# Second expert layer: an up-projection by seven products of halves instead of eight, on pairs of blocks

## The chip, the cores and the metric

The kernel runs on one core of one Trainium2 chip. The metric is the device time of one execution in microseconds, smaller is better. Three executions of the kernel before took 954.00, 954.44 and 953.73 us, median 954.0. The profiled execution took 954.2 us, with a span of 952.0 us from its first to its last instruction and a granted TensorE clock of 1.000 all the way.

## The reference

```python
q_p, k_p = phi(q * scale), phi(k * scale)        # exp of random features, 4 batches, 8 heads, 576 tokens
num = einsum('bhsm,bhmd->bhsd', q_p, einsum('bhsm,bhsd->bhmd', k_p, v))
den = einsum('bhsm,bhm->bhs', q_p, sum(k_p))[..., None] + 1e-06
x = (num / den), heads side by side               # 2304 tokens x 512
h = x @ moe_w_in                                  # first layer, 512 -> 2048
x = maximum(0.01 * h, h) @ moe_w_out              # 2048 -> 512
h = x @ moe2_w_in                                 # second layer, 512 -> 2048: the change is here
out = (h * clip(h + 3, 0, 6) / 6) @ moe2_w_out    # 2048 -> 512
```

All arrays are float32. Only `h` of the second layer, for token groups of 512, is computed in another way after the change.

## The kernel before

**Precision.** Every matrix product of the two layers is made from operands that are split into a high part, rounded to the type `F32R`, and a low part, the rest. `mm3` (L415 to L418) adds three matmuls: high by high, low by high, high by low. `copy_alts` makes the high part (ScalarE or VectorE, recorded at L409 and L408), `sub_alts` the low part (VectorE or GpSimd, L412 and L413).

**Groups and blocks.** The 2304 tokens are five groups, `GN = [512, 256, 512, 512, 512]`. Layer one takes them in this order, with the attention of the next group between the matmuls; layer two takes them as 0, 2, 3, 4, 1, so that the group of 256 is last. In `moe` (L715) a group goes over `FT` = 16 blocks of 128 hidden columns. `Hblk(j)` (L727) is the up-projection of a block: for each of the four slices of 128 input features (`xs[k]`, the split input) one `mm3` with the block's weights standing and the group's tokens moving, 12 matmuls into one PSUM bank. In layer two ScalarE then computes relu(h + 3) into a tile `u` (L742), VectorE computes min(u, 6) * h into the bank (L743), and the result is split into the two parts of `g` (L409, L748). `Oblk(j)` (L752) is the down-projection: `g` stands, the split `moe2_w_out` moves, 12 matmuls of 512 columns into four accumulator banks, two blocks behind `Hblk`. After the last block the four accumulators go through a scaled copy (`late_o`, L773) to the output.

**Weights.** `weight` (L435) loads one block of 512 KB by DMA into one of two buffers `wst`, turns 64-bit into 32-bit floats with four instructions (L444, L446, L449, L452), and splits it into a pair of tiles `w`. The split weights of a layer stay in SBUF for all five groups: 32 pairs of `w` are needed in each layer; seven further pairs (`NMORE`) become free when attention is over (`phase4`, L390), together with four output tiles `o`.

**The order of work.** Nothing is ordered by hand. Each operation goes to `Graph` with its possible engines and their planned costs, its buffers, and a due time. `Graph.run` repeatedly takes the operation that can start first by its own clock of the engines (due times decide between starts less than 60 ns apart), and writes the instructions in that order. An engine's cost is raised by `BIAS` when the planner chooses between engines (VectorE by 900 ns). Buffers of one tag are taken in the order of the program. Up-projection banks (`use` "H") may hold four of the eight PSUM banks at the end, accumulators (`acc`) four.

Of the kernel before, what the change touches and what calls it, by code (L numbers as in the profile page):

```python
# [24 lines left out]
KT = DM // 128  # L25
# [7 lines left out]
NMORE = 7  # L33
# [7 lines left out]
LEAD = 0.8  # L41
O1, O2 = 11e3, 12e3
EARLY2 = 60e3
T0, D1, D2 = 42e3, 100e3, 89e3
# [10 lines left out]
class Buf:  # L55
    __slots__ = ("tag", "slot", "left", "freed", "writers", "readers", "tiles", "first", "use", "phase")
    NOW = 0

    def __init__(self, tag, use=None):
# [9 lines left out]
class Graph:  # L69
# [6 lines left out]
    ANY = ("nm",)  # L76
    WHILE = {}
# [8 lines left out]
    def op(self, alts, rd=(), wr=(), due=0.0, also=()):  # L86
# [27 lines left out]
        for x in list(wr) + [(b, "new") for b in also]:  # L114
# [7 lines left out]
            if b.slot is None and b.tag is not None:  # L122
                b.slot = -1
                o.allocs.append(b)
                self.fifo.setdefault(b.tag, []).append(o.seq)
# [13 lines left out]
    def run(self, slots, spare, phase, later):  # L139
# [9 lines left out]
        turn = {t: 0 for t in self.fifo}  # L149
        held = {"acc": 0, "H": 0, "att": 0, "first": 0}  # L150
# [8 lines left out]
        while pend:  # L159
            best = None  # L160
            short = set()
            for o in sorted(pend, key=lambda o: (o.due, o.seq)):
# [5 lines left out]
                for b in o.allocs:  # L168
# [50 lines left out]
            for b in o.allocs:  # L219
# [9 lines left out]
                else:  # L229
                    turn[b.tag] += 1  # L230
            fn()
            done += 1
            for b in o.bufs:
                b.left -= 1
                b.freed = max(b.freed, o.end)
                if b.left == 0 and b.tag is not None:
# [3 lines left out]
                    if b.use is not None:  # L240
                        held[b.use] -= 1
            self.todo[o.phase] -= 1
# [58 lines left out]
def attn_moe_kernel(ctx: ExitStack, tc: tile.TileContext, qT, kT, qn, kn, v1, om2, w1i, w1o, w2i, w2o, out):  # L301
# [21 lines left out]
    x1 = [[dram.tile([128, GN[i]], F32, name=f"x1_{i}_{k}") for k in range(KT)] for i in range(NG)]  # L323
# [14 lines left out]
        "o": [],  # L338
# [75 lines left out]

    def mm3(o, ah, al, bh, bl, start, stop):  # L415
# [19 lines left out]
    def weight(src, j, due):  # L435
        st, t, w = Buf("wst"), Buf("wt"), Buf("w")
# [14 lines left out]
            rd=[(st, 1)], wr=[(st, 0)], due=due)  # L451
        g.op([("dve", c_dve(512), lambda: nc.vector.scalar_tensor_tensor(  # L452
# [262 lines left out]
    def moe(grp, second, wi, wo, T):  # L715
        n = GN[grp % NG]
        step = (D2 if second else D1) * n / 512.0 / (FT + 1.0)
        xs = [] if second or grp else [firstx[k] for k in range(KT)]
        for k in range(KT - len(xs)):
            xr, x = xraw[grp, k], Buf("x")  # L720
            g.op(copy_alts(lambda x=x: x.tiles[0][:, :n], lambda xr=xr: xr.tiles[0][:, :n], n), rd=[xr], wr=[(x, 0)], due=T - 1e3)
            g.op(sub_alts(lambda x=x: x.tiles[1][:, :n], lambda xr=xr: xr.tiles[0][:, :n], lambda x=x: x.tiles[0][:, :n], n), rd=[xr, (x, 0)],
                 wr=[(x, 1)], due=T - 1e3)
            xs.append(x)
        acc = [Ps("acc") for _ in range(n // 128 if second else KT)]

        def Hblk(j):  # L727
            p = Ps("H")
            P = lambda: p.tiles[0][:, :n]
            for k in range(KT):  # L730
                def mm(k=k):
                    wh, wl = win(wi[j], k)
                    mm3(P(), wh, wl, xs[k].tiles[0][:, :n], xs[k].tiles[1][:, :n], k == 0, k == KT - 1)
                g.op([("pe", 3 * c_mm(n), mm)], rd=[wi[j], xs[k]], wr=[p], due=T + step * (j - LEAD * (j == FT - 1)))
# [17 lines left out]
        def Oblk(j, gg):  # L752
            w = wo[j]
            for i, a in enumerate(acc):
                def mm(i=i, a=a):
                    c = slice(i * 128, i * 128 + 128)
                    if second:
                        mm3(a.tiles[0], gg.tiles[0][:, c], gg.tiles[1][:, c], w.tiles[0], w.tiles[1], j == 0, j == FT - 1)
                    else:
                        mm3(a.tiles[0][:, :n], w.tiles[0][:, c], w.tiles[1][:, c], gg.tiles[0][:, :n], gg.tiles[1][:, :n], j == 0, j == FT - 1)  # L760
                g.op([("pe", 3 * c_mm(512 if second else n), mm)], rd=[w, gg], wr=[a], due=T + step * (j + 1.6))

        gs = {}
        for j in range(FT + 2):
# [4 lines left out]
        for i, a in enumerate(acc):  # L769
            d = T + step * (FT + 1.0) - 4e3  # L770
            if second:
                o = Buf("o")
# [159 lines left out]
```

## Time and profile before

| | |
|---|---|
| median of three executions | 954.0 us (953.73 to 954.44) |
| the profiled execution | 954.2 us, span 952.0 us |
| TensorE busy | 945.0 us, 99% |
| weight loads on TensorE busy (beside matmuls) | 776.1 us |
| VectorE busy | 429.9 us, 45% |
| ScalarE busy | 423.4 us, 44% |
| GpSimd busy | 203.2 us, 21% |

In the profile, an instruction's time is its start to its end. Matmuls are pipelined: the time of one matmul reaches over the start of the next, so the distance from start to start is what a matmul takes from the engine. The same holds in smaller measure for the other engines. PE is TensorE, PEld its weight loads, DVE VectorE, ACT ScalarE, POOL GpSimd.

### The profile page before, as it was taken

The page shows a single profiled execution, that of the slowest core. Times are in us where ns is not written, and L with a number is a line of the kernel's source. Part 1 is how long each engine was busy: PE and PEld are TensorE (multiplying, and loading weights), DVE is VectorE, ACT ScalarE, POOL GpSimd, SP SyncE. Part 2 cuts the span into 40 slices and gives each one's busy share as a digit, 9 for nine tenths or more (in the row PEclk, how much of TensorE's full clock was granted, in tenths as well). Part 3 has the DMA queues.
Part 4 walks back from the last instruction along what each step waited for, and adds up shares of the span by engine and source line. Part 5 has one row for each costly group of instructions (what it writes and reads, how often), then busy time and mean ns, then how long its engine had stood idle before and what let it go on. Part 6 is the DMA issues. An engine that isn't in the chain of part 4 may idle for free.

```text
span 952.0 us, 13570 instructions
## 1 busy us (share of the span) xinstructions
PE 945.0 (99%) x5102; PEld 776.1 (82%) x5102; DVE 429.9 (45%) x1020; ACT 423.4 (44%) x964; POOL 203.2 (21%) x297
## 2 busy tenths in 40 slices
PE   9999999999999999999999999999999999999998
PEld 8878778899778877777888888888888888888897
DVE  6897978635722234124666663222222222222232
ACT  6867767655643344234545553232223223222332
POOL 2455445322410022012533421020002001000100
PEclk9999999999999999999999999999999999999999
DMA  9457545433201211000544450020002000100000
GB/s 328 131 160 233 186 141 156 117 91 97 64 26 55 60 45 56 1 1 1 199 133 133 123 187 22 1 89 1 1 0 89 1 1 11 55 1 1 29 17 23
DMA packets 38128, 72.92 MB, mean 77 GB/s; under 512 B 10032, under 2 KB 15280, under 8 KB 38064
## 3 DMA queue, kind: packets, MB, share of 16 engines
q1 hardware_dynamic: 38064, 72.07, 23.7%
q8 instruction: 40, 0.66, 0.3%
q14 instruction: 24, 0.20, 0.1%
HBM read 62.62 MB, written 9.44 MB: 76 GB/s over the span
## 4 chain that ended last, share of the span: by engine, by line
PE 97%; ACT 1%; DMA 1%; DVE 0%; issue 0%; SPq 0%; POOL 0%
PE bank L416 29%; PE bank L417 28%; PE bank L418 28%; PE bank L532 4%; PE bank L578 3%; PE bank L708 2%; PE bank L685 1%; PE bank L589 1%; PE bank L619 1%; ACT first_h L512 1%; DMA first_xn<-kn 1%; PE bank L553 0%; PE bank L610 0%; PE bank L637 0%; ACT ht L512 0%
## 5 line engine op out<-in xcount | busy, mean ns | idle before, releaser
L748 DVE TENSOR_TENSOR g<-bank,g 128x512 fp32r<-128x512 f32 (+1 forms) x160 | 101.7, 636 | 159.1 <-ACT g L409 158.3
L743 DVE SCALAR_TENSOR_TENSOR bank<-u,bank 128x512 f32<-128x512 f32 (+1 forms) x80 | 51.3, 642 | 230.0 <-ACT u L742 229.7
L742 ACT ACTIVATE u<-bank,three 128x512 f32<-128x512 f32 (+1 forms) x80 | 51.6, 645 | 198.2 <-PE bank L418 197.8
L416 PE MATMUL bank<-x,w 128*128 128x512 f32 (+1 forms) x340 | 127.3, 375 | 0.0
L418 PE MATMUL bank<-x,w 128*128 128x512 f32 (+1 forms) x340 | 125.3, 369 | 0.0
L417 PE MATMUL bank<-x,w 128*128 128x512 f32 (+1 forms) x340 | 125.2, 368 | 0.0
L409 ACT CAST g<-bank 128x512 fp32r<-128x512 f32 (+1 forms) x160 | 87.3, 546 | 50.9 <-DVE bank L743 49.4
L413 POOL TENSOR_TENSOR x<-xr,x 128x512 fp32r<-128x512 f32 (+1 forms) x36 | 42.5, 1203 | 309.7 <-ACT x L409 258.2
L746 ACT ACTIVATE bank<-bank 128x512 f32<-128x512 f32 (+1 forms) x80 | 43.7, 546 | 85.0 <-PE bank L418 84.2
L416 PEld LDWEIGHTS bank<-x,w 128*128 128x128 f32 x340 | 64.0, 188 | 15.1 <-issue 3.6
L416 PE MATMUL bank<-x,second_w 128*128 128x512 f32 (+1 forms) x200 | 76.0, 380 | 0.0
L501 DVE TENSOR_REDUCE nm<-bank 128x4 f32<-128x512 f32 (+3 forms) x92 | 49.5, 568 | 55.8 <-PE bank L532 55.0
L417 PE MATMUL bank<-x,second_w 128*128 128x512 f32 (+1 forms) x200 | 74.6, 373 | 0.0
L418 PE MATMUL bank<-x,second_w 128*128 128x512 f32 (+1 forms) x200 | 74.5, 373 | 0.0
L418 PEld LDWEIGHTS bank<-x,w 128*128 128x128 f32 x340 | 64.0, 188 | 10.9
L417 PEld LDWEIGHTS bank<-x,w 128*128 128x128 f32 x340 | 64.1, 188 | 10.6
L512 ACT ACTIVATE h<-bank,nm 128x128 f32<-128x128 f32 x208 | 58.6, 391 | 31.4 <-POOL nm L507 31.2
L416 PE MATMUL bank<-w,g 128*128 128x512 f32 x180 | 70.2, 390 | 0.0
L417 PE MATMUL bank<-w,g 128*128 128x512 f32 x180 | 70.2, 390 | 0.0
L418 PE MATMUL bank<-w,g 128*128 128x512 f32 x180 | 70.0, 389 | 0.0
L416 PE MATMUL bank<-g,w 128*128 128x512 f32 (+1 forms) x180 | 68.8, 382 | 0.0
L418 PE MATMUL bank<-g,w 128*128 128x512 f32 (+1 forms) x180 | 66.4, 369 | 0.0
(168 smaller groups left out, 1897.6 us busy)
## 6 DMA issues: line engine op xcount, KB each, us to landing
wst<-w2i SPq DMA_DIRECT2D x16, 512.0 KB, 3.6
wst<-w2o SPq DMA_DIRECT2D x16, 512.0 KB, 3.6
v<-v SPq DMA_DIRECT2D x14, 330.0 KB, 2.9
wst<-w1i SPq DMA_DIRECT2D x9, 512.0 KB, 4.8
wst<-w1o SPq DMA_DIRECT2D x9, 512.0 KB, 3.9
out<-late_o SPq DMA_DIRECT2D x18, 256.0 KB, 2.1
x<-u SPq DMA_DIRECT2D x16, 256.0 KB, 2.1
xr<-x SPq DMA_DIRECT2D x16, 256.0 KB, 2.8
```

The lines of the kernel that those rows point to most:

```text
L409: return [("act", c_act(n, psum), lambda: nc.scalar.copy(dst(), src())), dve if psum else dve + (True,)]
L413: ("pool", c_pool(n), lambda: nc.gpsimd.tensor_tensor(out=dst(), in0=src(), in1=hi().bitcast(F32), op=ALU.subtract))]
L416: nc.tensor.matmul(o, lhsT=ah, rhs=bh, start=start, stop=False)
L417: nc.tensor.matmul(o, lhsT=al, rhs=bh, start=False, stop=False)
L418: nc.tensor.matmul(o, lhsT=ah, rhs=bl, start=False, stop=stop)
L501: g.op([("dve", c_dve(c * 128), lambda raw=raw, n_=n_: nc.vector.tensor_reduce(out=n_()[:, :, 0], in_=raw(), axis=AX.X, op=ALU.min))], rd= ...
L512: nc.scalar.activation(h.tiles[0][:, q * 128:q * 128 + 128], raw()[:, q], AF.Exp, bias=nm.tiles[0][:, q], scale=-1.0)
L532: nc.tensor.matmul(ps[bank].tiles[0][o, i * 128:i * 128 + 128], lhsT=src.tiles[0][r, i * 128:i * 128 + n], rhs=wn[r], start=True, stop=True)
L742: g.op([("act", c_act(n, True, True), lambda: nc.scalar.activation(U(), P(), AF.Relu, bias=three))], rd=[p], wr=[u], due=d)
L743: g.op([("dve", c_dve(n), lambda: nc.vector.scalar_tensor_tensor(out=P(), in0=U(), scalar=6.0, in1=P(), op0=ALU.min, op1=ALU.mult))], rd=[ ...
L746: g.op([("act", c_act(n, True), lambda: nc.scalar.activation(P(), P(), AF.Prelu, alpha=0.01))], wr=[p], due=d)
L748: g.op([("dve", c_dve(n), lambda: nc.vector.tensor_tensor(out=G1(), in0=P(), in1=G0().bitcast(F32), op=ALU.subtract))], rd=[p, (gg, 0)], w ...
```

## The change

It concerns layer two alone, and there the four groups of 512 tokens (`fast`). Two blocks of hidden columns become a pair. The input (4 slices of 128 features by 512 tokens) and the pair's weights (4 slices by 256 hidden columns) are regarded as 2 x 2 matrices of halves: features halved into two slices each, tokens halved into 256 each, hidden columns halved into the two blocks. The four halves of the result come from seven products and a number of sums and differences, in place of eight products. Each product is two slices of `mm3` with 256 moving columns, that is, six matmuls. The sums are distributed thus:

- Input: for each group, four differences (`minus`) and seven splits (`xsplit`) replace four splits. Three of the split halves (`x2`) lie in `w` buffers.
- Weights: blocks of `moe2_w_in` stay unsplit (`raw`, two blocks to a buffer, in the space that attention leaves). For each pair in each group four sums or differences of 256 columns (`S`, in a `wst` buffer) and four splits (`c`, three of 512 columns and one of 256, in `w` buffers) are made anew. In the last group, of 256 tokens, each block is split anew as well, and its products stay as they were.
- Results: products that go into more than one half of the result are copied out of PSUM (`keep`) or added on the way out (`total`). Region `R[0]`, half a bank, is accumulated into by four products in turn, and is copied out after each of them, before the next may add to it.

```diff
-NMORE = 7
+NMORE = 3
+PAIRLAG = 2.0
+BIAS2 = 300.0
+EARLY3 = 20e3
+    CAP = {"c": 8, "x2": 3, "g2": 2}
...
-                    elif t not in self.ANY and self.fifo[t][turn[t]] != o.seq:
+                    elif t not in self.ANY and self.fifo[b.line][turn[b.line]] != o.seq:
+                        ok = None
+                        break
+                    elif lines[b.line] >= self.CAP.get(b.line, 99):
...
             if left == 0:
                 share["H"], share["att"], share["first"] = HSHARE, 0, 0
+                self.BIAS = dict(self.BIAS, dve=BIAS2)
...
-        a, x = room("late", [("o", 4, ([128, 512], F32)), ("w", NMORE, *wspec)], 0, side="right")
+        a, x = room("late", [("raw", FT // 2, ([128, 512], U32), ([128, 512], U32)), ("u", NMORE, ([128, 512], F32))], 0, side="right")
...
+    def add_alts(dst, a, b, n, op):
+        return [("dve", c_dve(n), lambda: nc.vector.tensor_tensor(out=dst(), in0=a(), in1=b(), op=op), True),
+                ("pool", c_pool(n), lambda: nc.gpsimd.tensor_tensor(out=dst(), in0=a(), in1=b(), op=op))]
...
+        if raw:
+            g.op([("dve", c_dve(512), lambda: nc.vector.scalar_tensor_tensor(
+                out=w.tiles[j % 2], in0=t.tiles[0], scalar=3, in1=low(), op0=ALU.logical_shift_left, op1=ALU.bitwise_or), True)],
+                rd=[t, (st, 0)], wr=[(w, j % 2)], due=due)
+            return w
...
+        def halves(b, src, rd, due, m=n):
+            g.op(copy_alts(lambda: b.tiles[0][:, :m], lambda: src()[:, :m], m), rd=rd, wr=[(b, 0)], due=due)
+            g.op(sub_alts(lambda: b.tiles[1][:, :m], lambda: src()[:, :m], lambda: b.tiles[0][:, :m], m), rd=rd + [(b, 0)], wr=[(b, 1)], due=due)
+            return b
+        def minus(to, a, b, due):
+            c = b if to is a else a
+            g.op(add_alts(lambda: to.tiles[0], lambda: a.tiles[0], lambda: b.tiles[0], 512, ALU.subtract), rd=[c], wr=[to], due=due)
...
+        if fast:
+            r11, r12, r21, r22 = (xraw[grp, k] for k in range(KT))
...
+            b11 = xsplit(r11, 0.0)
+            minus(r11, r12, r11, T - 8e3)
+            b21 = xsplit(r21, 1e3)
+            t1 = xsplit(r11, 2e3, line="x2")
+            minus(r12, r22, r12, T - 6e3)
+            minus(r11, r22, r11, T - 6e3)
+            t2 = xsplit(r11, 4e3, line="x2")
+            t3 = xsplit(r12, 5e3, line="x2")
+            b22 = xsplit(r22, 6e3)
+            minus(r21, r21, r11, T - 3e3)
+            t4 = xsplit(r21, 7e3)
...
+        def Hpair(j):
+            raw, t0 = wi[j], T + step * j
+            d = t0 - 7e3
+            ra, rb = lambda: raw.tiles[0].bitcast(F32), lambda: raw.tiles[1].bitcast(F32)
+            S = Buf("wst", line="S")
+            part = lambda i: S.tiles[0].bitcast(F32).rearrange("p a b -> p (a b)")[:, i * 256:i * 256 + 256]
+            c = [Buf("w", line="c") for _ in range(4)]
+            halves(c[0], ra, [(raw, 0)], d, 512)
+            g.op(add_alts(lambda: part(0), lambda: rb()[:, 0:256], lambda: rb()[:, 256:512], 256, ALU.add), rd=[(raw, 1)], wr=[(S, 0)], due=d)
+            g.op(add_alts(lambda: part(1), lambda: part(0), lambda: ra()[:, 0:256], 256, ALU.subtract), rd=[(raw, 0), (S, 0)], wr=[(S, 1)], due=d)
+            g.op(add_alts(lambda: part(2), lambda: ra()[:, 0:256], lambda: rb()[:, 0:256], 256, ALU.subtract), rd=[raw], wr=[(S, 2)], due=d)
+            g.op(add_alts(lambda: part(3), lambda: ra()[:, 256:512], lambda: part(1), 256, ALU.subtract), rd=[(raw, 0), (S, 1)], wr=[(S, 3)], due=d)
+            both = lambda i: S.tiles[0].bitcast(F32).rearrange("p a b -> p (a b)")[:, i * 256:i * 256 + 512]
+            halves(c[1], lambda: both(0), [(S, 0), (S, 1)], d + 1e3, 512)
+            halves(c[2], lambda: both(2), [(S, 2), (S, 3)], d + 2e3, 512)
+            halves(c[3], lambda: rb()[:, 256:512], [(raw, 1)], d + 3e3, 256)
+            p, q = Ps("H"), Ps("H")
+            R = [lambda: p.tiles[0][:, 0:256], lambda: q.tiles[0][:, 0:256], lambda: q.tiles[0][:, 256:512]]
+            bank = [(p, 0), (q, 0), (q, 1)]
+            def prod(r, a, off, b, at, start, also=()):
+                def mm():
+                    for k in range(2):
+                        w = [c[a].tiles[h][:, off + k * 128:off + k * 128 + 128] for h in range(2)]
+                        m = [b.tiles[h][:, k * 256:k * 256 + 256] for h in range(2)]
+                        for i, (x, y) in enumerate(((0, 0), (1, 0), (0, 1))):
+                            nc.tensor.matmul(R[r](), lhsT=w[x], rhs=m[y], start=start and k == i == 0, stop=k == 1 and i == 2,
+                                             skip_group_check=True)
+                g.op([("pe", 6 * c_mm(256), mm)], rd=[c[a], b], wr=[bank[r]], also=also, due=t0 + step * at)
+            s, h0, h1 = Buf("u", line="s"), Buf("u", line="h"), Buf("u", line="h")
+            hold = lambda i: s.tiles[0][:, i * 256:i * 256 + 256]
+            def keep(i, at):
+                g.op(copy_alts(lambda: hold(i), R[0], 256, True), rd=[bank[0]], wr=[(s, i)], due=t0 + step * at - 6e3)
+            def total(h, half, r, i, at):
+                g.op([("dve", c_dve(256), lambda: nc.vector.tensor_tensor(
+                    out=h.tiles[0][:, half * 256:half * 256 + 256], in0=hold(i), in1=R[r](), op=ALU.add))],
+                    rd=[bank[r], (s, i)], wr=[(h, half)], due=t0 + step * at - 6e3)
+            prod(0, 0, 0, b11, 0.0, True)
+            prod(1, 0, 256, b21, 0.1, True)
+            keep(0, 0.1)
+            prod(2, 1, 0, t1, 0.2, False, [])
+            total(h0, 0, 1, 0, 0.2)
+            prod(0, 1, 256, t2, 0.5, False)
+            keep(1, 0.5)
+            prod(0, 2, 0, t3, 0.9, False)
+            keep(0, 0.9)
+            total(h1, 1, 2, 0, 0.9)
+            prod(0, 3, 0, t4, 1.3, False)
+            g.op(copy_alts(lambda: h1.tiles[0][:, 0:256], R[0], 256, True), rd=[bank[0]], wr=[(h1, 0)], due=t0 + step * 1.3 - 6e3)
+            prod(2, 2, 256, b22, 1.4, False)
+            total(h0, 1, 2, 1, 1.4)
+            out = []
+            for h, u, gg in ((h1, p, Buf("g")), (h0, q, Buf("w", line="g2"))):
+                U, X = lambda u=u: u.tiles[0], lambda h=h: h.tiles[0]
+                d = t0 + step * 1.9 - 6e3
+                g.op([("act", c_act(512, False, True), lambda U=U, X=X: nc.scalar.activation(U(), X(), AF.Relu, bias=three))], rd=[h], wr=[u], due=d)
+                g.op([("dve", c_dve(512), lambda U=U, X=X: nc.vector.scalar_tensor_tensor(
+                    out=X(), in0=U(), scalar=6.0, in1=X(), op0=ALU.min, op1=ALU.mult))], rd=[u], wr=[h], due=d)
+                out.append(halves(gg, X, [h], d, 512))
...
+            if second:
+                w = halves(Buf("w", line="c"), lambda: wi[j].tiles[j % 2].bitcast(F32), [(wi[j], j % 2)], T + step * j - 6e3, 512)
...
+        for j in range(0, FT + 2, 2) if fast else ():
+            if j < FT:
+                gs[j + 1], gs[j] = Hpair(j)
+            if j >= 2:
+                Oblk(j - 1, gs.pop(j - 1), PAIRLAG - 1.0)
+                Oblk(j - 2, gs.pop(j - 2), PAIRLAG + 1.0)
```

The layer between (`x1` in DRAM) is laid out so that a half of the tokens of two slices can be loaded into one tile.

## Rows read from the trace of the kernel before

**Rows 1.** The page: busy time of the engines, and the chain that ended last.
```profile
PE 945.0 (99%) x5102; PEld 776.1 (82%) x5102; DVE 429.9 (45%) x1020; ACT 423.4 (44%) x964; POOL 203.2 (21%) x297
PE 97%; ACT 1%; DMA 1%; DVE 0%; issue 0%; SPq 0%; POOL 0%
```

**Rows 2.** Waits of PE, whole run, longest first: us in total, times, longest.
```profile
PE bank L637 <- DVE u L628: 1.1, 1, 1.1
...
PE bank L532 <- DMA first_xT<-qT: 0.2, 1, 0.2
```

**Rows 3.** Stretches of layer two: us, busy PE, PEld, DVE, ACT, POOL, PEclk, DMA share, GB/s.
```profile
550.00:638.25 88.25, 88.25 (x386) 72.09 (x384) 35.21 (x53) 33.73 (x55) 15.55 (x12) 1.00 0.19 61
638.25:726.53 88.28, 88.28 (x386) 72.12 (x384) 22.19 (x32) 24.80 (x41) 5.07 (x4) 1.00 0.07 24
903.09:952.00 48.91, 45.18 (x289) 40.66 (x287) 13.65 (x32) 15.44 (x36) 0.00 (x0) 1.00 0.08 29
```

**Rows 4.** Timeline, one up-projection block of 512 columns: start us, us, engine, line.
```profile
762.50 0.39 PE L416 MATMUL bank<-x,w 128*128 128x512 f32 x1
762.51 0.19 PEld L417 LDWEIGHTS bank<-x,w 128*128 128x128 f32 x1
...
765.22 0.39 PE L416 MATMUL bank<-w,g 128*128 128x512 f32 x1
```

**Rows 5.** Timeline of PE in the group of 256 tokens.
```profile
903.09 0.28 PE L416 MATMUL bank<-x,late_w 128*128 128x256 f32 x1
...
906.65 0.39 PE L416 MATMUL bank<-late_w,g 128*128 128x512 f32 x1
...
908.04 0.28 PE L416 MATMUL bank<-x,late_w 128*128 128x256 f32 x1
```

**Rows 6.** Groups of DVE by form: busy us, mean ns, idle before.
```profile
L748 DVE TENSOR_TENSOR g<-bank,g 128x512 fp32r<-128x512 f32 x128 | 88.2, 690 | 134.8 <-ACT g L409 134.0
...
L743 DVE SCALAR_TENSOR_TENSOR bank<-u,bank 128x512 f32<-128x512 f32 x64 | 44.4, 696 | 202.4 <-ACT u L742 202.3
...
L748 DVE TENSOR_TENSOR g<-bank,g 128x256 fp32r<-128x256 f32 x32 | 13.5, 422 | 24.3 <-ACT g L409 24.3
```

**Rows 7.** Timeline of DVE while layer-two weights are prepared.
```profile
474.37 0.68 DVE L748 TENSOR_TENSOR g<-bank,g 128x512 fp32r<-128x512 f32 x1
474.97 0.68 DVE L452 SCALAR_TENSOR_TENSOR wt<-wt,wst 128x512 uint32<-128x512 uint32 x1
...
476.90 1.06 DVE L446 TENSOR_SCALAR wst<-wst 128x512 uint32<-128x512 uint32 x1 [1.25 <-ACT wt L444]
```

**Rows 8.** Groups of ACT by form.
```profile
L409 ACT CAST g<-bank 128x512 fp32r<-128x512 f32 x128 | 75.1, 587 | 42.7 <-DVE bank L743 41.4
L742 ACT ACTIVATE u<-bank,three 128x512 f32<-128x512 f32 x64 | 44.0, 688 | 178.1 <-PE bank L418 177.9
...
L409 ACT CAST g<-bank 128x256 fp32r<-128x256 f32 x32 | 12.2, 382 | 8.2 <-DVE bank L743 7.9
```

**Rows 9.** Timeline of ACT: three copies from SBUF in a row.
```profile
451.69 1.66 ACT L409 CAST x<-xr 128x512 fp32r<-128x512 f32 x3
```

**Rows 10.** Stretches within attention, columns as before.
```profile
40.00:150.00 110.00, 108.92 (x626) 86.34 (x626) 92.70 (x220) 74.21 (x174) 54.66 (x64) 1.00 0.57 179
150.00:250.00 100.00, 100.00 (x820) 87.64 (x819) 61.11 (x234) 60.44 (x186) 37.33 (x80) 1.00 0.36 105
```

**Rows 11.** Timeline of all engines: GpSimd beside the DVE instruction at 476.90.
```profile
476.38 1.29 POOL L413 TENSOR_TENSOR w<-wt,w 128x512 fp32r<-128x512 f32 x1 [2.94 <-ACT w L409]
```

**Rows 12.** Timeline: a result handed from ACT to DVE.
```profile
760.04 0.69 ACT L742 ACTIVATE u<-bank,three 128x512 f32<-128x512 f32 x1 [3.40 <-PE bank L418]
...
760.76 0.70 DVE L743 SCALAR_TENSOR_TENSOR bank<-u,bank 128x512 f32<-128x512 f32 x1 [3.40 <-ACT u L742]
```

**Rows 13.** The page: DMA issues, with KB each and us to landing.
```profile
wst<-w2i SPq DMA_DIRECT2D x16, 512.0 KB, 3.6
```

More of the change, by code (lines that the diff above doesn't have):

```diff
@@ L55, with __init__ @@
 class Buf:
-    __slots__ = ("tag", "slot", "left", "freed", "writers", "readers", "tiles", "first", "use", "phase")
+    __slots__ = ("tag", "slot", "left", "freed", "writers", "readers", "tiles", "first", "use", "phase", "line")
     NOW = 0
-    def __init__(self, tag, use=None):
+    def __init__(self, tag, use=None, line=None):
+        self.line = line or tag
         self.tag, self.slot, self.left, self.freed, self.use = tag, None, 0, 0.0, use
@@ L124, in op @@
                 o.allocs.append(b)
-                self.fifo.setdefault(b.tag, []).append(o.seq)
+                self.fifo.setdefault(b.line, []).append(o.seq)
         for b, s in norm:
@@ L149, in run @@
         turn = {t: 0 for t in self.fifo}
+        lines = {t: 0 for t in self.fifo}
         held = {"acc": 0, "H": 0, "att": 0, "first": 0}
@@ L229, in run @@
                 else:
-                    turn[b.tag] += 1
+                    turn[b.line] += 1
+                    lines[b.line] += 1
             fn()
@@ L241, in run @@
                         held[b.use] -= 1
+                    else:
+                        lines[b.line] -= 1
             self.todo[o.phase] -= 1
@@ L321, in many @@
         return [tuple(sb(f"{name}{i}_{j}", *s, pool=pool) for j, s in enumerate(specs)) for i in range(n)]
-    x1 = [[dram.tile([128, GN[i]], F32, name=f"x1_{i}_{k}") for k in range(KT)] for i in range(NG)]
+    x1 = [[dram.tile([128, 2, GN[i]], F32, name=f"x1_{i}_{k}") for k in range(KT // 2)] for i in range(NG)]
     stage = [("wst", ([128, 512, 2], U32)), ("wt", ([128, 512], U32))]
@@ L717, in moe @@
         step = (D2 if second else D1) * n / 512.0 / (FT + 1.0)
+        fast = second and n == 512
         xs = [] if second or grp else [firstx[k] for k in range(KT)]
[L719 to L724, printed above, removed]
@@ new lines, in moe @@
+        if fast:
+            r11, r12, r21, r22 = (xraw[grp, k] for k in range(KT))
+            xsplit = lambda r, d, **line: halves(Buf("w" if line else "x", **line), lambda: r.tiles[0], [r], T - 9e3 + d)
+            b11 = xsplit(r11, 0.0)
[9 more added lines that the diff above has]
+            t4 = xsplit(r21, 7e3)
+        else:
+            for k in range(KT - len(xs)):
+                xs.append(halves(Buf("x"), lambda xr=xraw[grp, k]: xr.tiles[0], [xraw[grp, k]], T - 1e3))
@@ new lines, in moe @@
+        acc = [Ps("acc") for _ in range(n // 128 if second else KT)]
+        first, last = (1, FT - 2) if fast else (0, FT - 1)
+        def Hpair(j):
[56 more added lines that the diff above has]
+                out.append(halves(gg, X, [h], d, 512))
+            return out
@@ L750, in Hblk, with Oblk @@
             return gg
-        def Oblk(j, gg):
+        def Oblk(j, gg, lag=0.0):
             w = wo[j]
@@ L757, in mm @@
                     if second:
-                        mm3(a.tiles[0], gg.tiles[0][:, c], gg.tiles[1][:, c], w.tiles[0], w.tiles[1], j == 0, j == FT - 1)
+                        mm3(a.tiles[0], gg.tiles[0][:, c], gg.tiles[1][:, c], w.tiles[0], w.tiles[1], j == first, j == last)
                     else:
-                        mm3(a.tiles[0][:, :n], w.tiles[0][:, c], w.tiles[1][:, c], gg.tiles[0][:, :n], gg.tiles[1][:, :n], j == 0, j == FT - 1)
-                g.op([("pe", 3 * c_mm(512 if second else n), mm)], rd=[w, gg], wr=[a], due=T + step * (j + 1.6))
+                        mm3(a.tiles[0][:, :n], w.tiles[0][:, c], w.tiles[1][:, c], gg.tiles[0][:, :n], gg.tiles[1][:, :n], j == first, j == last)
+                g.op([("pe", 3 * c_mm(512 if second else n), mm)], rd=[w, gg], wr=[a], due=T + step * (j + 1.6 + lag))
         gs = {}
-        for j in range(FT + 2):
+        for j in range(0, FT + 2, 2) if fast else ():
[4 more added lines that the diff above has]
+                Oblk(j - 2, gs.pop(j - 2), PAIRLAG + 1.0)
+        for j in () if fast else range(FT + 2):
             if j < FT:
@@ L771, in moe @@
             if second:
-                o = Buf("o")
+                o = Buf("u", line="o")
                 g.op([("act", c_act(512, True), lambda a=a, o=o: nc.scalar.mul(o.tiles[0], a.tiles[0], 1.0 / 6.0)),
@@ L808, in weights @@
                 Buf.NOW = 0 if grp else 1 if i < NW1 else 2 if i < 2 * FT - 3 * ST2 // 2 else 0
-                d.append(weight(s, j, SG[grp] + step * (j + o) - 4e3 - (EARLY2 * (FT - j) / FT if grp else 0.0)))
+                raw = None if not grp or o else d[-1] if j % 2 else Buf("raw")
+                d.append(weight(s, j, SG[grp] + step * (j + o) - 4e3 - (EARLY2 * (FT - j) / FT + EARLY3 if grp else 0.0), raw))
         Buf.NOW = 0
```

22 lines of the change are left out of this document (14 added, 8 removed).

## The prediction

> **What bounds the kernel now.** I read the shares of the engines first: TensorE is busy 99% of the span, and 97% of the chain that ended last is TensorE [rows 1]. Busy matmul time overlaps itself, so next I asked for TensorE's waits: six in the whole run, the longest 1.1 us, the shortest 0.2, and none of them in layer two [rows 2]. Then the stretches of layer two. A group of 512 tokens takes 88.25 to 88.28 us, four times, at a granted clock of 1.00 (2.4 GHz); VectorE and ScalarE are busy about a quarter of that [rows 3]. A group has 384 matmuls of 512 columns (16 blocks, 12 up and 12 down), so one costs 88.28 / 384 = 0.2299 us of TensorE. Layer two is a gapless stream of matmuls, and its time is their number times the distance between two starts. What an added vector instruction costs is nothing, until TensorE waits for it.
>
> **Matmuls: what seven products save.** Before, two blocks take 24 up-projection matmuls of 512 columns. After, 7 products x 2 slices x 3 split parts = 42 of 256 columns, the work of 21. This holds only if 256 columns cost half of 512. The trace has that shape in the group of 256 tokens: 30 of them lie between 903.09 and 906.65 [rows 5], 3.56 / 30 = 0.1187 us each. Twice that is 0.2374, or 3% over 0.2299; so of one eighth (12.5%) 9.6% is left. Per pair: 24 x 0.2299 - 42 x 0.1187 = 5.518 - 4.985 = 0.532 us. There are 8 pairs in each of 4 groups: **-17.0 us**. Bounds: 512 columns take 2.72 / 12 = 0.2267 us in one stretch [rows 4] and 1.39 / 6 = 0.2317 in another [rows 5]; with these the saving is 14.6 or 18.4 us. The down-projection and the last group keep their matmuls.
>
> Each 256-column matmul still loads 128 weight columns. A load takes 0.19 us and starts 0.01 us after the start of the matmul before it, while that runs [rows 4]; the loads are hidden at either length, as the 0.1187 already contains. The Trainium skill (TensorE: Matmul & The Clock Gate, section "Part 3: Packing small matmuls — row/col tiling") speaks against this change: a weight load overlaps a running matmul only when it goes to another group of rows. All of these loads use all rows, so by that rule they would stand in line, and more, shorter matmuls would lose; the rivals price it.
>
> **Added vector work.** Distances between starts: VectorE 0.60 us for 512 columns, from 474.37 to 474.97 [rows 7], where the duration is 0.69 [rows 6]. I take the same 0.09 off the 0.42 of 256 columns: 0.33 (an estimate). ScalarE: three copies of 0.62 in 1.66 us, that is (1.66 - 0.62) / 2 = 0.52 each [rows 9]; 0.10 less than the duration, so 0.28 for a copy of 256 and 0.59 for the relu [rows 8]. Per pair, with all that VectorE or GpSimd could do on VectorE:
> - low parts: 5 of 512 (3 weight, 2 g) and 1 of 256; sums of weights: 4 of 256; totals: 3 of 256; min-times: 2 of 512. Together 7 x 0.60 + 8 x 0.33 = 6.85 us.
> - ScalarE: high parts 5 x 0.52 and 0.28, four copies out of PSUM of 0.28, two relus of 0.59: 5.2 us.
>
> A pair's matmuls take 4.985 + 24 x 0.2299 = 10.50 us. So VectorE is at 65%, ScalarE at 50%. Per group come four differences and seven splits of the input, 11 x 0.60 = 6.6 us on VectorE and 3.6 on ScalarE: 73% and some 56% over a group of 84 us. Is that hidden? In attention the same planner keeps TensorE at 108.9 of 110 us with VectorE at 84%, and at 100 of 100 with VectorE at 61% and ScalarE at 60% [rows 10]. Steady state: 0, and it is TensorE that is full.
>
> **Switches of group.** The seven split inputs have one set of buffers. Each is free only when the last pair of the old group has used it, and is wanted one pair later. In that 10.5 us VectorE is asked for 6.85 + 6.6 = 13.5 us: 3.0 too many. GpSimd can help less than its idle time suggests: VectorE's instruction at 476.90 took 1.06 us, until just after GpSimd's of 476.38 to 477.67 ended [rows 7, 11]. Against the 3.0 us stand the weights (3 x 0.60 + 5 x 0.33 = 3.45 us a pair), which may be made a pair ahead (`c` has eight buffers), and the results, wanted two pairs later. I take 0.5 us a switch, four times: **+2.0** (bounds 0 and 3.0 each).
>
> The Trainium skill (SBUF — State Buffer, section "Who interferes with whom") calls this an exclusive lock: a VectorE instruction with two SBUF inputs, or one in a mode that uses both ports, blocks against a GpSimd instruction that reads SBUF. By that rule only the totals and min-times, which read PSUM, run beside GpSimd, and the 3.0 us remain to be covered by lookahead; without it GpSimd (1.3 us each) could take three of the eleven and leave 1.2.
>
> **The hand-over of the region R[0].** Four products add into the same half bank, each after the one before was copied out. A hand-over is the matmul's end behind the next possible start (0.28 - 0.12 = 0.16) [rows 5], a copy of 0.38 [rows 8] and two signals of 0.03 (760.04 + 0.69 to 760.76 [rows 12]): 0.60 us. The first is covered by two products of 0.71 us on other regions; the next two of each pair need down-projection matmuls between (0.69 for three, eight such triples a pair). Within a group there are always some, since they lag two pairs. Only at the start of layer two are there few: the last two blocks of layer one (5.5 us) cover one pair, the second pair pays two hand-overs, 1.2 us, and I add 0.8 for its weights: **+2.0** (bounds 0 and 5). No row shows a bank that is read in one half while matmuls write the other. Taken as 0, as reads of other banks cost nothing [rows 4, 12]; at most seven reads a pair of 0.38 to 0.42 us, 2.8 us a pair.
>
> **At nothing.** The loads: two stage buffers, 3.6 us from issue to landing [rows 13], now shared with the sums `S`; the split weights of the down-projection wait for buffers that layer one frees, where seven more were free before. In the first stretch the tail of the loads is still there (DMA 0.19, VectorE 35.2 of 88 us [rows 3]). But a pair uses up its two blocks only every 10.5 us, so the last ones are wanted 73 us after the first. Without this cover: some 4 us, one load from issue to landing. The last group splits 16 blocks anew, 0.60 on VectorE and 0.52 on ScalarE each; its block lasts 12 x 0.1187 + 6 x 0.2299 = 2.80 us with VectorE busy under a third [rows 3]: nothing. Layer one and attention keep their work.
>
> **Sum.** Profiled span 952.0 - 17.0 + 2.0 + 2.0 = 939.0; with the 2.2 us around the span (954.2 - 952.0) 941.2. That execution lies 0.2 above the median of 954.0. Forecast: **941 us**.
>
> **Rivals.**
> 1. *Forecast*: TensorE stays the bound, with small gaps at switches. 936 to 945. Chance 0.60.
> 2. *The switches are not hidden*: three entries into a group of 512 at 3.0 us and 5 at the start of layer two: 954.2 - 17.0 + 14 = 951; half hidden 945. For it: 13.5 us of work for 10.5. Against: weights ahead, results behind, TensorE fed at 84% VectorE. 0.20.
> 3. *Slower: hand-overs in the open.* The planner takes whatever starts first, so down-projection triples may be spent before they are needed as cover, or a copy stands in ScalarE's queue behind a weight copy that waits for VectorE. 2 x 32 = 64 hand-overs x 0.60 = 38.4 us, 975.6 if all are open. It decides from 17.0 / 38.4 = 44% open, or 0.27 us waited on average. For it: ScalarE and VectorE are first-in first-out and twice as full as now. Against: eight triples for two gaps. 0.12, with the half-bank conflict beside it (up to 2.8 x 32 = 90 us) 0.02 more.
> 4. *Loads in line* (the rule above): 18 more loads of 0.19 a pair less the 0.53: +2.9 x 32 = 92 us, 1046. The rows refute it at both lengths: 0.01.
> 5. *Better*: no gap at all and 18.4 saved: 935.8 or below. 0.05.
>
> **How the numbers follow.** About 0.2% (1.9 us) can be told from no change. Faster by more: all of 1 and 5, 0.17 of 2: 0.82. Within: 0.03 of 2 and 0.01 of 3: 0.04. Slower: 0.14. The range leaves out most of 5, the end of 2 above 953 and 3 and 4: 935 to 953.
>
> **What would show it.** Right: starts of 256-column matmuls in the new product groups 0.118 to 0.119 apart; a group of 512 lasting 84 to 85 us, not 88.28; matmuls 5102 + 18 x 32 = 5678; VectorE busy above 600 us and ScalarE above 530; TensorE's waits in layer two a few us, at the four switches. Wrong: many waits of TensorE for ScalarE's copies out of the bank, all through the groups (rival 3); gaps that pile up only at group starts (rival 2); product matmuls more than 0.125 apart (half-bank). The prediction falls if a group lasts over 88 us.

## The result, and the profile after

The changed kernel takes 940.62 us (median of four executions, 940.18 to 940.93) against 954.0: a ratio of 0.9859, interval 0.9842 to 0.9876. Its profiled span is 938.9 us, 13.1 less than before; the forecast had 941 us and a span of 939.0.

The page of the changed kernel, busy time and the chain that ended last, as in [rows 1]:

```profile
PE 930.2 (99%) x5678; PEld 787.5 (84%) x5678; DVE 593.8 (63%) x1373; ACT 520.3 (55%) x1207; POOL 239.5 (26%) x349
PE 96%; ACT 1%; DVE 1%; DMA 0%; issue 0%; SPq 0%; POOL 0%
```

There are 5678 matmuls, 576 more than before and yet 15 us less busy: TensorE is still the bound, and 164 us more of VectorE and 97 us more of ScalarE lie beside it. TensorE's waits over the whole run have one entry in layer two (L806 is the matmul of the products, L817 `total`):

```profile
PE bank L806 <- DVE late_u L817: 0.7, 1, 0.7
```

The first stretch of layer two and a later one, columns as in [rows 3]:

```profile
550.00:643.00 93.00, 92.21 (x587) 82.28 (x586) 84.63 (x156) 61.02 (x125) 32.73 (x32) 1.00 0.24 80
643.00:728.00 85.00, 85.00 (x530) 75.21 (x530) 62.15 (x110) 51.24 (x106) 30.13 (x31) 1.00 0.08 27
```

The later one is the steady state: VectorE 73% busy, GpSimd 35%, and TensorE without a pause. In the first VectorE is at 91%, since the last weights are still being converted, and TensorE loses 0.8 us of busy time. Three output transfers of layer two, the last one of a group each, give the length of a group:

```profile
643.46 0.33 SPq L905 DMA_DIRECT2D out<-u  x1
...
728.41 0.33 SPq L905 DMA_DIRECT2D out<-late_u  x1
...
813.02 0.33 SPq L905 DMA_DIRECT2D out<-u  x1
```

85.0 and 84.6 us, where it was 88.28.

**Where the 13.1 us come from.** I took the distances from start to start of all recorded matmuls of layer two. Products: 118.5 ns (256-column matmuls before: 118.6). Matmuls of 512 columns: 231.5 ns, before 230.0. With 864 + 768 = 1632 of 512 columns before and 864 after, and 192 + 1344 = 1536 of 256 after, the streams are 1632 x 0.2300 + 192 x 0.1186 = 398.1 us and 864 x 0.2315 + 1536 x 0.1185 = 382.0 us: 16.1 us saved. Distances over 12 ns longer than these add 3.1 us after and none before: 1.9 us before 643, then 0.6, 0.4 and 0.3 us in the next groups. 16.1 - 3.1 = 13.0.

**One hand-over.** The timeline of a steady pair, between two products of region R[0] (the three matmuls of one `mm3` of the down-projection, a triple, stand between them):

```profile
739.51 0.87 PE L806 MATMUL bank<-second_w,second_w 128*128 128x256 f32 x6
...
740.22 0.39 PE L436 MATMUL bank<-w,g 128*128 128x512 f32 x1
...
740.42 0.37 ACT L422 COPY late_u<-bank 128x256 f32<-128x256 f32 x1 [3.14 <-PE bank L806]
...
740.68 0.40 PE L438 MATMUL bank<-w,g 128*128 128x512 f32 x1
...
740.84 0.76 PEld L806 LDWEIGHTS bank<-x,w 128*128 128x128 f32 x6 [0.20 <-ACT late_u L422]
740.92 0.90 PE L806 MATMUL bank<-x,w 128*128 128x256 f32 x6
```

The product that starts at 739.51 gives TensorE over at 740.22. ScalarE copies the region from 740.42 to 740.79, and the weight load of the next product is released at 740.84: 0.62 us after TensorE was free, for 0.60 forecast. The down-projection triple between lasts 0.70 us (740.22 to 740.92) and covers it, with 0.08 us to spare; the matmul of the product starts at 740.92. The first matmul after the load that waited takes 0.150 us to the next start, not 0.118; these 0.03 us return in each pair.

### The profile page after: what moved, and what is told of

Same layout as the page of the kernel before. It is cut to its first block, busy times and chain, and to the rows that moved or that the text cites. A ratio compares the mean times of both kernels' runs of the same rounds, so it can differ in the third digit from the quotient of the medians.

```text
span 938.9 us, 15330 instructions
## 1 busy us (share of the span) xinstructions
PE 930.2 (99%) x5678; PEld 787.5 (84%) x5678; DVE 593.8 (63%) x1373; ACT 520.3 (55%) x1207; POOL 239.5 (26%) x349
## 4 chain that ended last, share of the span: by engine, by line
PE 96%; ACT 1%; DVE 1%; DMA 0%; issue 0%; SPq 0%; POOL 0%
PE bank L436 23%; PE bank L437 22%; PE bank L438 22%; PE bank L806 17%; PE bank L558 4%; PE bank L604 3%; PE bank L734 2%; PE bank L711 1%; PE bank L615 1%; PE bank L645 1%; ACT first_h L538 1%; DMA first_xn<-kn 0%; PE bank L579 0%; PE bank L636 0%; PE bank L663 0%
## 5 line engine op out<-in xcount | busy, mean ns | idle before, releaser
L869 DVE TENSOR_TENSOR g<-bank,g 128x512 fp32r<-128x512 f32 (+1 forms) x96 | 57.5, 599 | 121.2 <-ACT g L422 120.4
L422 ACT COPY late_u<-bank 128x256 f32<-128x256 f32 (+1 forms) x103 | 38.9, 380 | 82.3 <-PE bank L806 80.5
L436 PE MATMUL bank<-x,w 128*128 128x512 f32 (+1 forms) x200 | 74.2, 371 | 0.0
L438 PE MATMUL bank<-x,w 128*128 128x512 f32 (+1 forms) x200 | 72.0, 360 | 0.0
L437 PE MATMUL bank<-x,w 128*128 128x512 f32 (+1 forms) x200 | 71.9, 360 | 0.0
L436 PE MATMUL bank<-g,w 128*128 128x512 f32 (+1 forms) x180 | 69.1, 384 | 0.0
L438 PE MATMUL bank<-g,w 128*128 128x512 f32 (+1 forms) x180 | 66.4, 369 | 0.0
L437 PE MATMUL bank<-g,w 128*128 128x512 f32 (+1 forms) x180 | 66.3, 368 | 0.0
L806 PEld LDWEIGHTS bank<-x,second_w 128*128 128x128 f32 x420 | 54.0, 188 | 4.3 <-ACT late_u L422 2.1
L806 PE MATMUL bank<-x,second_w 128*128 128x256 f32 x420 | 57.2, 281 | 0.0
L436 PE MATMUL bank<-x,second_w 128*128 128x512 f32 (+1 forms) x156 | 56.2, 360 | 0.0
L437 PE MATMUL bank<-x,second_w 128*128 128x512 f32 (+1 forms) x156 | 54.8, 352 | 0.0
L438 PE MATMUL bank<-x,second_w 128*128 128x512 f32 (+1 forms) x156 | 54.8, 351 | 0.0
L422 ACT CAST g<-bank 128x512 fp32r<-128x512 f32 (+1 forms) x95 | 49.4, 520 | 8.8 <-DVE bank L864 6.4
L436 PE MATMUL bank<-w,g 128*128 128x512 f32 x120 | 47.2, 394 | 0.0
L437 PE MATMUL bank<-w,g 128*128 128x512 f32 x120 | 47.2, 393 | 0.0
L438 PE MATMUL bank<-w,g 128*128 128x512 f32 x120 | 46.9, 391 | 0.0
L436 PEld LDWEIGHTS bank<-x,w 128*128 128x128 f32 x200 | 37.7, 188 | 9.9 <-issue 3.0
```

The costliest lines, as they stand in the source:

```text
L422: return [("act", c_act(n, psum), lambda: nc.scalar.copy(dst(), src())), dve if psum else dve + (True,)]
L436: nc.tensor.matmul(o, lhsT=ah, rhs=bh, start=start, stop=False)
L437: nc.tensor.matmul(o, lhsT=al, rhs=bh, start=False, stop=False)
L438: nc.tensor.matmul(o, lhsT=ah, rhs=bl, start=False, stop=stop)
L806: nc.tensor.matmul(R[r](), lhsT=w[x], rhs=m[y], start=start and k == i == 0, stop=k == 1 and i == 2, skip_group_check=True)
L869: g.op([("dve", c_dve(n), lambda: nc.vector.tensor_tensor(out=G1(), in0=P(), in1=G0().bitcast(F32), op=ALU.subtract))], rd=[p, (gg, 0)], w ...
```

## The experiments

Every time is beside the kernel before on the same chip (953.4 to 953.8, against 954.0 beside the changed kernel). Differences named below are to the 940.62 us of the changed kernel, so one of less than about 1 us says nothing.

**Splitting anew, without the seven products.**

```diff
-        fast = second and n == 512
+        fast = False
...
-            if n == 512:
+            if False:
```

> Layer two's weights stay unsplit and are split anew for each group, as in the changed kernel, but all groups use eight products (384 matmuls of 512 columns in a group). Theory (the matmul stream is the bound, vector work is hidden): the saving of 17.0 us goes and the new splitting costs nothing, so groups of 88.3 us and 954 to 956 us, no wait of TensorE in layer two. Rival (the splitting anew is what costs the 4 us that the changed kernel lost against the pure matmul saving): 957 to 960 us, with groups over 89 us.

953.53 us, ratio 0.9999 (0.9990 to 1.0008), and no wait of TensorE in layer two. The same stretch as above:

```profile
643.00:728.00 85.00, 85.00 (x371) 69.40 (x370) 33.66 (x53) 30.82 (x52) 1.33 (x1) 1.00 0.06 20
```

VectorE is at 40% for 25% before, and nothing of it shows. The splitting anew costs nothing at this load of VectorE; the whole change of the time is in the products and what hangs on them.

**More vector work, on the products' path and off it.** In the first kernel the low parts of a pair's weights are made twice, in the second six differences are added whose results nothing waits for (they do keep the buffer `c[3]` in use until they are done).

```diff
             halves(c[3], lambda: rb()[:, 256:512], [(raw, 1)], d + 3e3, 256)
+            for _ in range(1):
+                for b, src, rd, m in ((c[0], ra, [(raw, 0)], 512), (c[1], lambda: both(0), [(S, 0), (S, 1)], 512),
+                                      (c[2], lambda: both(2), [(S, 2), (S, 3)], 512), (c[3], lambda: rb()[:, 256:512], [(raw, 1)], 256)):
+                    g.op(sub_alts(lambda b=b, m=m: b.tiles[1][:, :m], lambda src=src, m=m: src()[:, :m], lambda b=b, m=m: b.tiles[0][:, :m], m)[:1],
+                         rd=rd + [(b, 0)], wr=[(b, 1)], due=d + 3e3)
```

> The changed kernel with each pair's four weight low parts computed a second time on VectorE (three of 512 columns, one of 256: 2.13 us more a pair, 68 us in all). Theory: hidden as long as VectorE's work fits under a pair's 10.5 us of matmuls (6.85 + 2.13 = 8.98 us, 86%, and 93% of a group with the input's splits): under +3 us, 941 to 944 us. Rival (VectorE at its 73 to 80% is already the limit at switches and in the first group): a third or more of the 68 us shows, over 960 us.

```diff
             total(h0, 1, 2, 1, 1.4)
+            for _ in range(6):
+                g.op(add_alts(lambda: c[3].tiles[1][:, 256:512], lambda: ra()[:, 0:256], lambda: rb()[:, 0:256], 256, ALU.subtract)[:1],
+                     rd=[raw], wr=[(c[3], 2)], due=t0 + step * 1.5)
```

> The changed kernel with six more differences of 256 columns a pair on VectorE (6 x 0.33 = 2.0 us, 63 us in all), made after the pair's sixth product into a part of a buffer that nothing reads. The same load as in the run with repeated weight low parts (2.13 us a pair, 975.8 us), but nothing waits for these results. Theory (what that run lost is VectorE's queue: later work stands behind the added work): 20 to 35 us more, 960 to 976 us, again most in the first two groups. Rival (it lost because the repeated splits lay ahead of the products that wait for them, not through occupancy): under 5 us more, 941 to 946 us.

975.79 us (+35.2) and 953.31 us (+12.7). The stretch 643 to 728 of the first, and of the second:

```profile
643.00:728.00 85.00, 76.25 (x461) 65.45 (x460) 78.05 (x129) 49.33 (x102) 37.49 (x34) 1.00 0.08 25
```

```profile
643.00:728.00 85.00, 81.74 (x505) 71.67 (x506) 80.04 (x160) 53.13 (x109) 35.93 (x32) 1.00 0.09 27
```

For the first run my theory (under 3 us) failed and the rival's number (over 960) came true; the second lies between its theory (960 to 976) and its rival (under 946). The load alone, 2.0 us a pair, costs a fifth of itself (12.7 of 63 us), with VectorE at 94% of the stretch; nearly the same load ahead of the products costs half (35.2 of 68). So occupancy is one part, and position, with what follows from it, the larger one. In the first run 17.8 of the 23.6 us of TensorE's waits in layer two are for VectorE (L822 is `total` in that file), the longest entries first:

```profile
PE bank L811 <- DVE u L822: 6.6, 7, 1.8
PE bank L436 <- ACT g L422: 4.1, 3, 2.1
PE bank L437 <- DVE g L425: 3.4, 7, 0.7
```

In its first group the granted clock of the stretch 550 to 643 is 0.94, after waits of TensorE of up to 2.1 us. Over the whole run it is 0.993, in the second run 1.00; an estimate from that, 0.007 x 974.7 = 6.8 us, is the most that the clock can have in the 35.2. How the rest divides between the queue and the products' own wait for the repeated parts was not tried.

**When the down-projection falls due.** `PAIRLAG`, the number of blocks by which the planner's due times hold the down-projection back, is -2.0 and 3.0 for 2.0.

> The changed kernel with PAIRLAG -2.0 for 2.0: down-projection triples fall due before the products of later pairs and are used as soon as they are ready, rather than held back. Theory of the hand-overs (each one that is not covered costs 0.60 us, 64 of them after the first of a pair): if the triples are spent too early, up to half of the 64 open up, 5 to 20 us more, 946 to 960 us, seen as waits of TensorE for the copies out of the bank. Rival (the planner covers hand-overs whatever the due times, since a triple is taken whenever a product is not ready): within 2 us of 940.6.

> The changed kernel with PAIRLAG 3.0 for 2.0: the down-projection falls due one block later still. Theory (at 2.0 every hand-over of the region is already covered by triples): no gain, 940 to 943 us. Rival (more triples held back close the small gaps of 0.03 to 0.1 us that recur in each pair): 939 us or less.

952.91 us (+12.3), as the theory had it, and 944.03 us (+3.4), which neither theory nor rival had. With -2.0 eight triples run in a row, and the products that follow have none between them. TensorE's timeline in a steady pair, products only:

```profile
746.10 0.88 PE L806 MATMUL bank<-second_w,third_w 128*128 128x256 f32 x6
747.80 0.97 PE L806 MATMUL bank<-second_w,w 128*128 128x256 f32 x6 [0.82 <-ACT u L422]
748.61 1.57 PE L806 MATMUL bank<-x,second_w 128*128 128x256 f32 x12
755.60 0.86 PE L806 MATMUL bank<-x,second_w 128*128 128x256 f32 x6
```

The product after 746.10 should start at 746.81 and starts at 747.80: an open hand-over of 0.99 us, of which the profile shows 0.82 as idle. It is longer than the 0.62 us of the steady pair above because the copy stands in ScalarE's queue behind a relu:

```profile
746.75 0.69 ACT L839 ACTIVATE bank<-u,three 128x512 f32<-128x512 f32 x1
...
747.38 0.36 ACT L422 COPY u<-bank 128x256 f32<-128x256 f32 x1
```

It starts 0.57 us after 746.81, where in the steady pair it starts 0.20 us after the product. From 750.0 to 755.6 the 24 matmuls of eight triples run without a break. The long distances of layer two add up to 15.6 us for 3.1. With 3.0 the steady groups have no more idle time than with 2.0; the loss is in the first stretch (TensorE busy 90.0 of 93 us for 92.2), and most of it in one place:

```profile
621.96 1.45 POOL L426 TENSOR_TENSOR w<-wst,w 128x512 fp32r<-128x512 f32 x1
622.21 1.75 DVE L425 TENSOR_TENSOR third_w<-xr,third_w 128x512 fp32r<-128x512 f32 x1
...
623.88 0.41 DVE L817 TENSOR_TENSOR late_u<-u,bank 128x256 f32<-128x256 f32 x1
...
624.35 0.98 PE L806 MATMUL bank<-x,w 128*128 128x256 f32 x6 [1.86 <-DVE late_u L817]
```

VectorE's low part lasts 1.75 us beside a GpSimd instruction (0.69 is usual), `total` stands behind it, and TensorE waits 1.86 us. Matmuls of 512 columns from 625.7 to 629.0 then start about 0.425 us apart, a granted clock of 0.93 over 620 to 643. Why the order of work came out so with 3.0 was not tried.

**Buffers for the input's sums.** `CAP` limits how many buffers one use may hold; `CAP["x2"]` is 6 for 3.

> The changed kernel with six buffers for the split sums of the input (x2) in place of three, so that three of the seven splits of a new group can be made before the last pair of the old group is done with its own. Theory (the switches between steady groups cost at most 0.5 us each): 939.5 to 940.8 us. Rival (13.5 us of work for 10.5 us shows up at the switches): 1.5 us or more back, under 939.2 us.

940.43 us, not distinguishable, as the theory had it. The switches between steady groups have nothing to give back.

**GpSimd off the second layer's splits and sums.** `add_alts` without its GpSimd alternative, and in `halves`:

```diff
+            alts = sub_alts(lambda: b.tiles[1][:, :m], lambda: src()[:, :m], lambda: b.tiles[0][:, :m], m)
+            g.op(alts[:1] if second else alts, rd=rd + [(b, 0)], wr=[(b, 1)], due=due)
```

> The changed kernel with GpSimd taken off the splits and sums of layer two: VectorE does them all (6.85 us of a pair's 10.5, and 73% of a group with the input's splits, by the durations of the prediction). Theory (VectorE alone has room in the steady groups, GpSimd's hold on it costs what it saves): 940 to 943 us, no wait behind a held VectorE. Rival (GpSimd's share is needed at the switches and in the first group, where VectorE is over its room): 945 to 955 us.

941.16 us, within the theory's range, and VectorE at 68.3 of 85 us in the steady stretch (62.2 with GpSimd's help). GpSimd's 30 us of busy time a group save VectorE 6 us, and TensorE nothing.

**Loads first, and who holds the stage buffers.** The up-projection blocks are loaded before the down-projection's; then the same with two ways to keep the sums `S` from the stage buffers.

```diff
-        for j in range(FT):
-            for s, d, o in ((si, di, 0.0), (so, do, 1.6)):
+        order = [(j, k) for j in range(FT) for k in range(2)] if not grp else [(j, k) for k in range(2) for j in range(FT)]
+        for j, k in order:
+            for s, d, o in (((si, di, 0.0), (so, do, 1.6))[k],):
```

> The changed kernel with layer two's sixteen up-projection blocks loaded before its sixteen down-projection blocks, in place of alternating. Theory (2 of the 4 us that were lost lie in the first group, where the last loads and conversions share stage buffers and VectorE with the pairs' sums): the loads end sooner, since unsplit blocks wait for no buffer of layer one, and 1 to 2 us come back: 939 to 940 us. Rival (the first group's gaps come from the switch between layers alone, whatever the loads): 940.3 to 941.

973.06 us, +32.4: the opposite of both. The timeline of the stage buffers `wst`, in order of time:

```profile
494.52 0.42 DVE L429 TENSOR_TENSOR wst<-late_raw 128x256 f32<-128x256 f32 x1
...
498.77 0.33 SPq L457 DMA_DIRECT2D wst<-w2i  x1
...
505.07 0.42 DVE L429 TENSOR_TENSOR wst<-late_raw 128x256 f32<-128x256 f32 x1
```

```profile
549.68 0.42 DVE L421 CAST w<-wst 128x512 fp32r<-128x512 f32 x1
...
553.21 0.62 ACT L422 CAST w<-wst 128x512 fp32r<-128x512 f32 x1
554.59 8.21 SPq L457 DMA_DIRECT2D wst<-w2i  x2
```

The sums of the third pair are written at 494.5 (the fourth's at 505.1) and read only from 549.7, when layer two begins to free the weight buffers that they are split into. Until then they hold both stage buffers, and no load is issued from 498.8 to 554.6. TensorE then waits for weights, and the granted clock falls to 0.68 and 0.66 in the stretches where it stands (the last two rows are its longest waits):

```profile
574.00:582.00 8.00, 0.90 (x6) 0.69 (x6) 6.46 (x12) 3.34 (x6) 0.00 (x0) 0.68 0.44 131
...
611.00:622.00 11.00, 0.36 (x2) 0.00 (x0) 8.73 (x16) 4.81 (x9) 0.00 (x0) 0.66 0.47 143
```

```profile
PE bank L806 <- ACT w L422: 10.7, 1, 10.7
PE bank L436 <- ACT second_w L422: 10.0, 3, 7.5
```

To show that this is the cause, a sum takes its stage buffer only together with two weight buffers (`also=c[1:3]` on the first sum), or at most one sum is in them (`CAP["S"] = 1`):

> The up-projection blocks loaded first, as in the run that took 973.1 us, together with the rule that a sum takes its stage buffer only with its two weight buffers. Theory (the 32 us of that run came from the sums of the third and fourth pair, which held both stage buffers from 494 and 505 us until layer two freed weight buffers at 550, so that no load was issued from 499 to 555): all of it goes, 938 to 941.5 us, the loads end before 585 us. Rival (the loads in this order wait for something else, such as the unsplit buffers or VectorE): over 950 us.

> The same limit of one sum in the stage buffers, with the up-projection blocks loaded first. Theory (the 973.1 us of that order came from both stage buffers held by sums): the loads go on without the hole of 56 us, through one buffer at worst, and the time is 940 to 947 us. Rival (one buffer is too few for sixteen loads of some 7 us each before they are wanted): over 955 us.

946.57 and 955.00 us, both slower than their theories had it. The first recovers 26.5 of the 32.4 us, with the loads of the down-projection from 504.5 to 582.1 us; the second, which leaves one buffer held, 18.1, and ends on its rival's bound (955). The held buffers are shown as the cause of most. The same two rules on the loads in their old order:

> The changed kernel, but the first sum into the stage buffer S also takes the two weight buffers c that its splits need, so that S never sits in a stage buffer while it waits for them. Theory (in the first group the sums and the last loads get in each other's way in the two stage buffers; about 2 us of the 4 us of gaps lie there): the loads end before 598 us and 0.5 to 2 us come back, 938.6 to 940.1 us. Rival (those gaps come from VectorE's load and GpSimd's hold on it at the start of layer two, not from the buffers): within 0.5 us of 940.6.

> The changed kernel with at most one sum S at a time in the two stage buffers, so that one is always left to the loads. Theory (the 11 us without a load from 535.7 to 547.1 and the slow loads after it come from sums in the stage buffers, and about 1 us of the first group's 2 us of gaps with them): loads end before 595 us, 939 to 940.2 us. Rival (sums a pair ahead are worth more than early loads, as the run in which a sum waited for its weight buffers, 945.8 us, suggests): 941 to 946 us.

945.82 us (+5.2) and 940.46 us (no difference), where the theories had both gain. The first also tells what was left above: with this rule the two orders of the loads differ by 0.75 us (946.57 and 945.82), which is not distinguishable, so what stayed there is about the price of the rule itself. The last load is issued at 597.4 and 598.6 us, in the changed kernel at 598.5. So the sums in the stage buffers are not what slows its loads, and what leaves two of them 11 us apart (535.7 and 547.1) stays open. The first of the two loses most of its time in the first stretch (TensorE busy 89.3 of 93 us for 92.2), with waits of this form, where VectorE takes 1.49 us for 256 columns (0.42 is usual) beside a GpSimd instruction of 1.76:

```profile
569.00 1.76 POOL L426 TENSOR_TENSOR w<-late_raw,w 128x512 fp32r<-128x512 f32 x1 [1.54 <-ACT w L422]
...
569.55 1.49 DVE L425 TENSOR_TENSOR third_w<-late_raw,third_w 128x256 fp32r<-128x256 f32 x1
...
571.56 0.41 DVE L817 TENSOR_TENSOR late_u<-late_u,bank 128x256 f32<-128x256 f32 x1
...
572.02 0.97 PE L806 MATMUL bank<-x,second_w 128*128 128x256 f32 x6 [1.05 <-DVE late_u L817]
```

No run beats the changed kernel by a difference that can be told from noise.

## Why the prediction was right, point by point

**What bounds, and the saving.** Right. TensorE's stream is the time, a 256-column matmul costs 118.5 ns for the 118.7 read off beforehand, and without the seven products all of the gain is gone (953.53). The saving came out at 16.1 for 17.0 us. The size that was off is the 512-column matmul: I held its distance at 0.2299, and it rose to 0.2315 in layer two, 864 x 0.0015 = 1.3 us. The rule on row groups (the Trainium skill, TensorE: Matmul & The Clock Gate, "Part 3: Packing small matmuls — row/col tiling") does not hold here: 576 more loads, each of all rows, ran under matmuls at these distances. The same section also names loads into a background weight buffer, which the prediction left out.

**Vector work in steady state: 0.** Right as a number: 73% was forecast for VectorE and 73% of the steady stretch is measured, although GpSimd took part of the work; on VectorE alone it is 80%. (For the whole run I had VectorE above 600 us and ScalarE above 530; they are at 594 and 520. ScalarE's terms for a group add up to 45.2 of 84 us, 54% and not the 56% given; 60% is measured.) The reason given for it was too comfortable. That TensorE was fed in attention with VectorE at 84% said little here: 2.0 us more a pair cost 12.7 us, and 2.13 us ahead of the products 35.2. What the added work costs is not the switches of rival 2 alone: the long distances add up to 6.2, 5.4, 3.1 and 1.2 us in the four stretches of the run with 2.0 us, against 1.9, 0.6, 0.4 and 0.3, and lie inside the groups too. By these two runs more hangs on whether the work is ahead of a product than on its amount.

**Switches of group: +2.0.** Too high. The three groups from 643 on lose 0.6, 0.4 and 0.3 us together with the hand-overs, and more buffers for the input's sums change nothing. So the 3.0 us were covered; that it was the lookahead that covered them is argued, since no run took it away.

**Start of layer two: +2.0.** Right in size, 1.9 us, but for another reason than given. The longest pause is not an open hand-over of the second pair; the timeline of the changed kernel at 597 shows it:

```profile
597.10 0.84 POOL L426 TENSOR_TENSOR third_w<-late_raw,third_w 128x256 fp32r<-128x256 f32 x1 [1.74 <-ACT third_w L422]
...
597.25 1.23 DVE L425 TENSOR_TENSOR third_w<-wst,third_w 128x512 fp32r<-128x512 f32 x1
...
598.40 0.41 DVE L817 TENSOR_TENSOR late_u<-late_u,bank 128x256 f32<-128x256 f32 x1
598.96 1.31 PE L806 MATMUL bank<-second_w,second_w 128*128 128x256 f32 x9 [0.75 <-DVE late_u L817]
```

VectorE's low part takes 1.23 us instead of 0.69 and ends at 598.48, 0.54 us after GpSimd's instruction (597.94); `total` behind it comes late, and TensorE waits 0.75 us, of which this delay can explain at most 0.54. That is the lock that the Trainium skill (SBUF — State Buffer, "Who interferes with whom") describes, and the trace agrees. With GpSimd off the time is no better: a pause of 1.0 us for VectorE stands in the same stretch. So here the lock only chose the place of a pause; with `PAIRLAG` 3.0, where it stood ahead of a `total`, it cost more.

**Hand-overs.** Right that triples cover them, and right in size: 0.62 us to the release of the next load, for 0.60. Rival 3 is real, in both of its forms: triples spent early cost 12.3 us, and the open hand-over shown took 0.99 us because a copy stood in ScalarE's queue as well. I had it at exactly nothing in steady state; a single triple of 0.70 us leaves 0.03 us a pair. Half banks read while the other half is written cost nothing that shows: the products kept their 118.5 ns.

**At nothing.** Right: TensorE has no wait for a load in layer two, and the group of 256 tokens, with its 16 blocks split anew, has none of the long distances.

So the mechanism and the signs were right, but that the sum met the span within 0.1 us is partly luck: the saving came out 0.9 us short, and the gaps 0.9 us short as well.

## What to carry to other kernels

Where TensorE runs without gaps, matmuls can be traded for vector work; price the shorter matmul by its distance between starts in the trace at hand. A free engine is not the test; ask what lies ahead of the next matmul in its queue, and keep independent matmuls in reserve for each place where an accumulator must be read before it is added to. A buffer shared between loads and intermediate results must not be given to a result that cannot yet go on.

## What was not expected of the hardware

Matmuls of 512 columns are not all alike. In layer two of the kernel before, the median from start to start is 227 ns where the operands lie in the first-allocated buffers (`x`, `g` and `w`), and 231 to 234 where one lies in a later pool (`second_w`, `late_w`), at the same clock of 1.00 and with nothing waiting; [rows 4] and [rows 5] show one of each. At 256 columns there is no such difference (117 to 121, before and after). The pool is not the whole of it: in the changed kernel the 360 matmuls of `g` against `w` have a median of 229 and a mean of 230.2 ns (three that wait left out), against a mean of 227.3 before under the same names, which alone comes to about 1 us. What sets the distance was not tried.
